# Six one-bank PSUM tiles for the block products of the last pair, and another order of VectorE's work there

## The chip, the cores and the metric

The kernel runs on one core of a Trainium2 chip. The metric is the device time of one execution in microseconds (us). Its engines are named as in the profile: PE (TensorE, matmuls; PEld is its weight load), DVE (VectorE), ACT (ScalarE), POOL (GpSimd) and SP (SyncE, which here only issues DMAs). PSUM, where PE leaves its results, has eight banks; one bank holds 512 fp32 numbers in each of the 128 partitions.

## The reference

For each of 8 batches and 12 heads an attention without softmax is computed, its heads are laid side by side to rows of 768, and a layer norm with a two-layer network and a residual follows:

```python
scores = scale * np.matmul(q, k.transpose(0, 1, 3, 2))     # q, k, v: (8, 12, 448, 64)
attn = np.maximum(scores, 0.0) ** 2 / S
x = np.matmul(attn, v)                                     # laid out as (8, 448, 768)
xn = (x - mu) / np.sqrt(var + 1e-06) * g_ln
ch = np.maximum(xn @ w_ch1, 0.0) @ w_ch2                   # 768 -> 3072 -> 768
out = x + ch
```

Inputs and output are fp32.

## The kernel before

The batches are worked on in four pairs; a pair has 896 tokens, seven tiles of 128. For each pair there is the attention (`scores`, `values`), the first layer (`ffn1`, 24 blocks of 128 hidden units, into `hT`) and the second layer (`ffn2`). The order of instructions is written out by hand: each engine works through its list in the order of the program text, and waits on semaphores for data and for buffers. For the pairs before the last, the second layer of one pair is interleaved with the attention of the next. PE is kept fed in this way almost without a gap.

The last pair has no attention to go with. There the second layer of six of its seven token tiles is computed by Strassen's scheme: `ffn2_pair` takes token tiles t and t + 4 as two block rows, the two halves of the 768 output columns as two block columns, and the two halves of the 3072 hidden units as the inner blocks. Seven block products of 12 matmuls (128x128 by 128x384) stand for eight. It is called for t = 0, 1 and 2, which are called rows here; `ffn2_last` does the token tile that is left, with 72 matmuls in three groups of 24. The sums of weight blocks (`w2_sum`) are made once; the sums of blocks of `hT` (`h_sum`, names s1, s2, s5, s6, s7) are made by DVE for one row ahead: `following("s1")` and its like issue, in the middle of one row, the sum that the next row needs, into the same tile.

The order of products in a row is 3, 2, 5, 4, 1, 6, 7. They go through PSUM as follows, with a and b for PSUM tiles:

- product 3 into a, which ACT copies to `d` (L733); product 2 into b, which DVE subtracts from `d` (L735);
- product 5 is added to what is in a, and ACT copies it to `c12` (L738); product 4 is added to b, and ACT copies it to `c21` (L742);
- product 1 into a new a; DVE makes `q_` = a + d (L745); POOL makes `d` - `c12` + `c21` (L746, L747);
- product 6 into a new b; DVE adds it to `q_` (L752); product 7 is added to a; DVE adds it to `d` (L757).

The four results of a row go through `result`: DVE scales and adds the residual in one instruction (L724), or, for `q_`, ACT scales (L727) and POOL adds (L728); `store` then issues two DMAs from SP's queue (L645) for each. The five fp32 tiles `z_sb` hold `d`, `c12`, `c21`, `q_` and the next row's `d`.

PSUM before is split for the whole kernel into two pools. `ps_sc` has three tiles of two banks (six banks) for the attention's scores and values; `ps_mm` has two tiles of one bank, for `ffn1`, `ffn2`, the seven products (m_ps) and `ffn2_last` (o_ps). In the last pair `ps_sc` is used last by `centre`, ahead of the fifth block of `ffn1`.

Of the kernel before, what the change touches and what calls it, by code (L numbers as in the profile page):

```python
# [28 lines left out]
def kernel(  # L29
# [22 lines left out]
    nc = tc.nc  # L52
    P = 128
    HP = 64
    bf16 = mybir.dt.bfloat16
    fp32 = mybir.dt.float32
# [13 lines left out]
    DH = d_model // 2  # L70
# [15 lines left out]
    hpool = ctx.enter_context(tc.tile_pool(name="h", bufs=1))  # L86
    opool = ctx.enter_context(tc.tile_pool(name="o", bufs=3))
    spool = ctx.enter_context(tc.tile_pool(name="stat", bufs=2))
    ps_sc = ctx.enter_context(tc.tile_pool(name="ps_sc", bufs=3, space=bass.MemoryType.PSUM))
    ps_mm = ctx.enter_context(tc.tile_pool(name="ps_mm", bufs=2, space=bass.MemoryType.PSUM))  # L90

    eps_sb = const.tile([P, 1], fp32)
# [215 lines left out]
    def of(blk, b=0):  # L308
        o = b % 2 * S
        return slice(o + blk[0] * HP, o + sum(blk) * HP)  # L310
# [93 lines left out]
    def centre(b, blk):  # L404
        w = blk[1] * HP
        if (b, blk) == FIRST:
            ps = ps_mm.tile([P, 512], fp32, tag="mm", name="sum_ps")[:, :w]
        else:
            ps = ps_sc.tile([P, 2, 512], fp32, tag="sc", name="sum_ps")[:, 0, :w]
        rows = [xT[b // 2][:, c, of(blk, b)] for c in range(K1)]  # L410
        if blk == FULL:
            rows = [part[b][:, i] for i in range(2)]
        for i, r in enumerate(rows):
            nc.tensor.matmul(ps, ones, r, start=(i == 0), stop=(i == len(rows) - 1))  # L414
        total = ps
        if (b, blk) != FIRST:
            total = spool.tile([P, S], fp32, tag="total", name="total_sb", bufs=1)[:, :w]
            nc.scalar.copy(total, ps)  # L418
        for c in range(K1):
            nc.vector.scalar_tensor_tensor(  # L420
                xc[b][:, c, of(blk)], total, g_mean[:, c:c + 1], xc[b][:, c, of(blk)],
                op0=ALU.mult, op1=ALU.add)
# [15 lines left out]
    def attention_block(b, blk):  # L438


        lo, hi, first = b * G, b * G + G, blk[0] == 0
        units = [lambda: transposed(lo)] if first else []

        def unit(n, part):
            squares_now()
            for i in range(4 * part, min(4 * part + 4, J), 2):
                scores(n, tuple(range(i, min(i + 2, J))), blk)
            if b == 1 and not first and part and n == hi - 1:
                transposed(hi)
            if part and n > lo:  # L450
                values(n - 1, blk)
                if not first:
                    load(n + 3, "v")
        for n in range(lo, hi):
            units.append(lambda n=n: unit(n, 0))
            if first and n + 1 < hi:
                units.append(lambda n=n: transposed(n + 1))
            units.append(lambda n=n: unit(n, 1))

        def last():  # L460
            values(hi - 1, blk)
            if b == 1 and not first:
                load(hi + 3, "v")
        units.append(last)
        units.append(lambda: centre(b, blk))
        return units
# [174 lines left out]
    def store(pair, t, cols, o, queues):  # L641
        for u, queue in enumerate(queues):
            b, j = divmod(2 * t + u, J)
            rows = out[2 * pair + b].rearrange("(p j) d -> j p d", j=J)[j]
            queue.dma_start(rows[:, cols], o[u * HP:(u + 1) * HP])  # L645
# [17 lines left out]
    def w2_sum_units():  # L663

        b = {(i, j): w2_part(i, j) for i in range(2) for j in range(2)}
        pairs = (
            ("t3", (0, 1), (1, 1), nc.vector.tensor_sub), ("t4", (1, 0), (0, 0), nc.vector.tensor_sub),
            ("t1", (0, 0), (1, 1), nc.vector.tensor_add), ("t6", (0, 0), (0, 1), nc.vector.tensor_add),
            ("t7", (1, 0), (1, 1), nc.vector.tensor_add))

        def unit(name, x, y, op, s):
            op(w2_sum[name][:, s], b[x][:, s], b[y][:, s])
        n = KH // 4
        return [lambda name=name, x=x, y=y, op=op, i=i: unit(name, x, y, op, slice(i * n, i * n + n))
                for name, x, y, op in pairs for i in range(4)]
# [23 lines left out]
    def ffn2_pair(pair, t, late, following):  # L699


        h = hT[pair].rearrange("p (kh k) (u s) -> p kh k u s", kh=2, s=P)
        left = dict(h_sum, s3=h[:, 0, :, t], s4=h[:, 1, :, t + 4])
        left["s2"], left["s5"] = h_sum["s2"], h_sum["s5"]

        def product(n, ps=None):
            first = ps is None
            if first:
                ps = ps_mm.tile([P, 512], fp32, tag="mm", name="m_ps")
            x, y = left[f"s{n}"], w2_sum[f"t{n}"]  # L710
            for ki in range(KH):
                nc.tensor.matmul(ps[:, :DH], x[:, ki], y[:, ki],  # L712
                                 start=(first and ki == 0), stop=(ki == KH - 1),
                                 skip_group_check=not first)
            return ps

        def fp():
            return late.tile([P, DH], fp32, tag="z", name="z_sb", bufs=5)

        def result(eng, z, row, half):  # L720
            u = t + 4 * row
            z3, x = z.rearrange("p (c d) -> p c d", d=D), xtok[pair][:, :, u, half * HP:(half + 1) * HP]
            if eng is nc.vector:
                eng.scalar_tensor_tensor(  # L724
                    z3, z3, rstd[pair][:, u:u + 1], x, op0=ALU.mult, op1=ALU.add)
            else:
                nc.scalar.mul(z, z, rstd[pair][:, u:u + 1])  # L727
                eng.tensor_add(z3, z3, x)  # L728
            store(pair, u, slice(half * DH, (half + 1) * DH), z, (nc.sync, nc.sync))

        a = product(3)
        d = fp()
        nc.scalar.copy(d, a[:, :DH])  # L733
        b = product(2)
        nc.vector.tensor_sub(d, d, b[:, :DH])  # L735
        product(5, a)
        c12 = fp()
        nc.scalar.copy(c12, a[:, :DH])  # L738
        product(4, b)
        following("s2")  # L740
        c21 = fp()
        nc.scalar.copy(c21, b[:, :DH])  # L742
        a = product(1)
        q_ = fp()
        nc.vector.tensor_add(q_, a[:, :DH], d)  # L745
        nc.gpsimd.tensor_sub(d, d, c12)  # L746
        nc.gpsimd.tensor_add(d, d, c21)  # L747
        result(nc.vector, c12, 0, 1)
        result(nc.vector, c21, 1, 0)
        b = product(6)  # L750
        following("s1")
        nc.vector.tensor_add(q_, q_, b[:, :DH])  # L752
        result(nc.gpsimd, q_, 1, 1)
        product(7, a)
        following("s6")
        following("s7")
        nc.vector.tensor_add(d, d, a[:, :DH])  # L757
        result(nc.vector, d, 0, 0)

    def ffn2_last(pair, t):  # L760
# [10 lines left out]
    def ffn1_units(b, blk=FULL):  # L771
        if blk == FULL:
            return [lambda ni=ni: ffn1(b, ni, blk) for ni in range(K2)]
        return [lambda: ffn1_head(b, blk)] + [lambda ni=ni: ffn1(b, ni, blk) for ni in range(3, K2)]
# [11 lines left out]
    def token_units(pair):  # L786
        return ([lambda: tokens(pair)] + [lambda t=t: statistics(pair, t) for t in range(NT)]
                + [lambda: roots(pair, 0, NT)])
# [6 lines left out]
    units, side = ffn1_units(0, BLK[0][0]), attention_block(0, BLK[0][1])  # L795
# [37 lines left out]
    units, side = ffn1_units(2 * pair), w2_sum_units()  # L833
    for i, unit in enumerate(units):
        if i == 4:
            centre(2 * pair + 1, FULL)
        unit()
        if i > 6:
            for _ in range(2):
                if side:  # L840
                    side.pop(0)()
    side = token_units(pair)
# [11 lines left out]
    for t in range(3):  # L854
        def following(name, t=t):
            if t < 2:
                h_sums_of(pair, t + 1, (name,), 0, KH)
        ffn2_pair(pair, t, late, following)
# [31 lines left out]
```

## Time and profile before

| | |
|---|---|
| median of 3 runs | 546.78 us (546.72, 546.78, 549.94) |
| profiled execution | 546.87 us |
| its span, first to last instruction | 545.0 us |
| granted TensorE clock, mean | 0.999 |
| PE busy | 533.3 us, 98% of the span |
| DVE busy | 300.2 us, 55% |
| ACT busy | 267.9 us, 49% |
| POOL busy | 119.6 us, 22% |
| products of the last pair, first matmul to first of o_ps | 487.69 to 533.29 us |

Busy time says how much of the span an engine had an instruction at work. Matmuls are pipelined: the length of one counts from its start to the end of its last result, so that two which follow each other overlap, and the pace is read from the starts. A row of the timeline gives the start, the length and the engine of a run of equal instructions, and in brackets how long the engine had been idle before, with what released it. The chain that ended last is a list of start, length, engine and line, followed back from the end of the kernel.

### The profile page before, as it was taken

The numbers are of one execution on the slowest core, as the hardware profiler recorded it, in microseconds if no ns is written. First come the engines' busy times: TensorE is split into PE (matmuls) and PEld (weight loads), VectorE is DVE, ScalarE is ACT, GpSimd is POOL, SyncE is SP. The second block draws the span as 40 slices with busy tenths as digits, with TensorE's granted clock in tenths as the row PEclk, the third lists the DMA queues.
The fourth block names the chain that finished last, engine by engine and source line by source line (L and its number), as shares of the span: only waits on it lengthen the run. The fifth ranks groups of instructions, "written<-read, shape, count | busy, mean of one in ns | idle before, by whom it ended". The sixth has DMA issues, their size and how long they took to land.

```text
span 545.0 us, 11195 instructions
## 1 busy us (share of the span) xinstructions
PE 533.3 (98%) x4720; PEld 315.5 (58%) x4720; DVE 300.2 (55%) x559; ACT 267.9 (49%) x440; POOL 119.6 (22%) x144
## 2 busy tenths in 40 slices
PE   8999999999999999999999999999999999999996
PEld 6677779655555555555555555555555555555555
DVE  5765752378886250057787432026687689035543
ACT  6967685555553444455545344445545244441110
POOL 7344111123526100003634400001230400001121
PEclk9999999999999999999999999999999999999999
DMA  9999999979999930029989980004831140001123
GB/s 197 206 205 208 211 171 185 168 126 160 164 152 146 167 42 1 0 55 147 163 149 134 176 109 1 1 14 88 151 75 31 44 102 1 1 0 26 34 58 88
DMA packets 111300, 56.64 MB, mean 104 GB/s; under 512 B 77330, under 2 KB 111250, under 8 KB 111250
## 3 DMA queue, kind: packets, MB, share of 16 engines
q0 software_dynamic: 26976, 25.50, 32.4%
q1 hardware_dynamic: 83490, 29.77, 31.8%
q8 instruction: 37, 0.61, 0.5%
q10 hardware_dynamic: 784, 0.66, 0.4%
q14 instruction: 13, 0.11, 0.1%
HBM read 51.91 MB, written 11.01 MB: 115 GB/s over the span
## 4 chain that ended last, share of the span: by engine, by line
PE 91%; DVE 2%; DMA 2%; POOL 2%; issue 1%; ACT 1%; POOLq 0%; DVEq 0%
PE h_ps L586 39%; PE o_ps L623 31%; PE sc_ps L331 7%; PE av_ps L361 6%; PE m_ps L712 5%; DMA w<-in_moe_w_ch_dram 2%; PE o_ps L766 1%; PE h_ps L608 1%; PE sum_ps L414 1%; DVE z_sb L724 1%; POOL z_sb L746 1%; ACT early L342 1%; PE tr_ps L216 0%; DVE h_sum L697 0%; POOL v_sb L126 0%
## 5 line engine op out<-in xcount | busy, mean ns | idle before, releaser
L586 PE MATMUL h_ps<-xc_sb,w 128*128 128x448 bf16 (+2 forms) x1368 | 218.9, 318 | 0.6 <-ACT early L342 0.3
L586 PEld LDWEIGHTS <-w 128*128 128x128 bf16 x1368 | 128.6, 98 | 86.6 <-issue 3.0
L623 PE MATMUL o_ps<-w,hT_sb 128*128 128x384 bf16 x1008 | 172.6, 326 | 0.0
L342 ACT ACTIVATE attn_sb<-sc_ps 128x896 bf16<-128x896 f32 (+4 forms) x150 | 126.4, 902 | 87.9 <-PE sc_ps L331 71.4
L594 ACT ACTIVATE hT_sb<-h_ps 128x448 bf16<-128x448 f32 (+2 forms) x213 | 103.0, 484 | 122.2 <-PE h_ps L586 121.7
L623 PEld LDWEIGHTS <-hT_sb 128*128 128x128 bf16 x1008 | 94.9, 98 | 74.7 <-issue 15.2
L344 DVE TENSOR_TENSOR attn_sb<-attn_sb 128x896 bf16<-128x896 bf16 x126 | 81.7, 654 | 40.2 <-ACT attn_sb L342 38.9
L565 DVE BATCH_NORM_STATS2 stats<-xtok_sb 128x6 f32<-128x384 bf16 x56 | 27.5, 533 | 34.3 <-DMA xtok_sb<-xT_sb 34.3
L397 POOL TENSOR_TENSOR part_sb<-part_sb,xT_sb 128x448 f32<-128x448 f32 x24 | 29.5, 1229 | 69.9 <-DVE xT_sb L368 62.3
L394 POOL TENSOR_TENSOR part_sb<-xT_sb 128x448 f32<-128x448 bf16 x6 | 6.6, 1105 | 172.9 <-DVE xT_sb L368 142.5
L571 DVE RECIPROCAL rstd_sb<-rstd_sb 128x1 f32<-128x1 f32 (+1 forms) x10 | 1.7, 168 | 72.4 <-ACT rstd_sb L570 72.4
L420 DVE SCALAR_TENSOR_TENSOR xc_sb<-total_sb,g_mean,xc_sb 128x448 bf16<-128x448 f32 (+2 forms) x54 | 29.0, 604 | 21.5 <-ACT total_sb L418 21.5
L634 DVE SCALAR_TENSOR_TENSOR o_sb<-o_ps,rstd_sb,xtok_sb 128x384 f32<-128x384 f32 (+1 forms) x45 | 27.0, 601 | 17.2 <-PE o_ps L623 11.0
L331 PE MATMUL sc_ps<-qT_sb,kT_sb 64*64 64x448 bf16 x504 | 35.0, 358 | 0.0
L368 DVE TENSOR_SCALAR xT_sb<-av_ps 128x896 bf16<-128x896 f32 (+2 forms) x30 | 27.0, 900 | 10.0 <-PE av_ps L361 9.8
L361 PE MATMUL av_ps<-attn_sb,v_sb 64*64 64x448 bf16 (+2 forms) x672 | 32.3, 327 | 0.0
L361 PEld LDWEIGHTS <-v_sb 64*64 64x64 bf16 x840 | 22.7, 107 | 11.9 <-issue 1.6
L384 DVE TENSOR_SCALAR xc_sb<-xT_sb,g_sb 128x448 bf16<-128x448 bf16 (+2 forms) x54 | 27.9, 567 | 1.0
L712 PEld LDWEIGHTS <-h_sum 128*128 128x128 bf16 x180 | 17.6, 98 | 12.9 <-issue 1.4
L331 PEld LDWEIGHTS <-kT_sb 64*64 64x64 bf16 x504 | 12.1, 105 | 17.6 <-issue 13.3
L126 POOL DMA_DIRECT2D v_sb<-in_v_dram x24 | 17.5, 730 | 20.2 <-PE av_ps L361 16.7
L746 POOL TENSOR_TENSOR z_sb<-z_sb 128x384 f32<-128x384 f32 x3 | 3.0, 998 | 81.7 <-DVE z_sb L745 81.7
(88 smaller groups left out, 335.8 us busy)
## 6 DMA issues: line engine op xcount, KB each, us to landing
out_dram<-o_sb SPq DMA_DIRECT2D x85, 96.0 KB, 3.0
v_sb<-in_v_dram POOLq DMA_DIRECT2D x24, 224.0 KB, 4.9
w<-in_moe_w_ch_dram POOLq DMA_DIRECT2D x12, 384.0 KB, 13.9
w<-in_moe_w_ch_dram POOLq DMA_DIRECT2D x4, 1152.0 KB, 20.0
q_sb<-in_q_dram POOLq DMA_DIRECT2D x20, 224.0 KB, 7.0
k_sb<-in_k_dram POOLq DMA_DIRECT2D x20, 224.0 KB, 5.7
out_dram<-z_sb SPq DMA_DIRECT2D x24, 96.0 KB, 2.2
hold_sb<-in_q_dram POOLq DMA_DIRECT2D x3, 224.0 KB, 11.9
```

The source lines that it names most:

```text
L331: nc.tensor.matmul(ps[cols, r, o * w:(o + 1) * w], g["k"](i)[rows, cols], g["q"](i, r)[rows, blk[0]:sum(blk), cols], start=True, stop=True)
L342: nc.scalar.activation(a, ps[:, :, :len(slots) * w], ACTF.Relu)
L344: nc.vector.tensor_mul(a, a, a)
L361: nc.tensor.matmul(ps[cols, hh, :w], v_sb[rows, pr, j * D:(j + 1) * D], g["attn"][i][rows, r, :], start=(j == 0), stop=(j == J - 1))
L384: nc.vector.tensor_scalar_mul(y, x, g_sb[:, c:c + 1])
L397: nc.gpsimd.tensor_add(part[b], part[b], x[:, c])
L420: nc.vector.scalar_tensor_tensor(xc[b][:, c, of(blk)], total, g_mean[:, c:c + 1], xc[b][:, c, of(blk)], op0=ALU.mult, op1=ALU.add)
L565: nc.vector.bn_stats(stats[:, n], xtok[pair][:, n * G:(n + 1) * G, t, :])
L586: nc.tensor.matmul(ps[:, :w], w1[:, c, ni * P:(ni + 1) * P], xc[b][:, c, of(blk)], start=(c == 0), stop=(c == K1 - 1))
L594: nc.scalar.activation(hT[pair][:, ni, o:o + w], ps[:, :w], ACTF.Relu)
L623: nc.tensor.matmul(ps[:, :DH], hT[pair][:, ki, t * P:(t + 1) * P], w2[:, ki, cols], start=(ki == 0), stop=(ki == K2 - 1))
L712: nc.tensor.matmul(ps[:, :DH], x[:, ki], y[:, ki], start=(first and ki == 0), stop=(ki == KH - 1), skip_group_check=not first)
```

## The change

- The pool `ps_sc` moves to the other end of PSUM and into an exit stack of its own, which is closed in the last pair right after `centre`. Its six banks become a pool `ps_m` with six tiles of one bank.
- Each row of `ffn2_pair` takes two tiles of `ps_m` for products 3, 2, 5 and 4, and two others for 1, 6 and 7, so that a row takes four, and the next row starts on the other two. `ffn2_last` keeps `ps_mm`.
- DVE's order within a row changes. Before: L745, `c12` (L724), `c21` (L724), s1, L752, s6, s7, L757, `d` (L724). After: L745, s1, L752, s6, `c12`, `c21`, L757, s7, `d`.
- The result `q_` (ACT L727, POOL L728, and its two stores on SP's queue) now stands ahead of the results `c12` and `c21` and their stores.

Line numbers are those of the kernel before.

```diff
-    ps_sc = ctx.enter_context(tc.tile_pool(name="ps_sc", bufs=3, space=bass.MemoryType.PSUM))
+    wide = ctx.enter_context(ExitStack())
+    ps_sc = wide.enter_context(
+        tc.tile_pool(name="ps_sc", bufs=3, space=bass.MemoryType.PSUM, side="right"))
...
-        def product(n, ps=None):
-            first = ps is None
-            if first:
-                ps = ps_mm.tile([P, 512], fp32, tag="mm", name="m_ps")
+        def banks():
+            return (ps_m.tile([P, 512], fp32, tag="m", name="m_ps")[:, :DH] for _ in range(2))
+
+        def product(n, ps, first=True):
...
-        a = product(3)
+        a, b = banks()
+        product(3, a)
         d = fp()
-        nc.scalar.copy(d, a[:, :DH])
-        b = product(2)
-        nc.vector.tensor_sub(d, d, b[:, :DH])
-        product(5, a)
+        nc.scalar.copy(d, a)
+        product(2, b)
+        nc.vector.tensor_sub(d, d, b)
+        product(5, a, False)
         c12 = fp()
-        nc.scalar.copy(c12, a[:, :DH])
-        product(4, b)
+        nc.scalar.copy(c12, a)
+        product(4, b, False)
         following("s2")
         c21 = fp()
-        nc.scalar.copy(c21, b[:, :DH])
-        a = product(1)
+        nc.scalar.copy(c21, b)
+        a, b = banks()
+        product(1, a)
         q_ = fp()
-        nc.vector.tensor_add(q_, a[:, :DH], d)
+        nc.vector.tensor_add(q_, a, d)
         nc.gpsimd.tensor_sub(d, d, c12)
         nc.gpsimd.tensor_add(d, d, c21)
+        following("s1")
+        product(6, b)
+        nc.vector.tensor_add(q_, q_, b)
+        result(nc.gpsimd, q_, 1, 1)
+        following("s6")
         result(nc.vector, c12, 0, 1)
         result(nc.vector, c21, 1, 0)
-        b = product(6)
-        following("s1")
-        nc.vector.tensor_add(q_, q_, b[:, :DH])
-        result(nc.gpsimd, q_, 1, 1)
-        product(7, a)
-        following("s6")
+        product(7, a, False)
+        nc.vector.tensor_add(d, d, a)
         following("s7")
-        nc.vector.tensor_add(d, d, a[:, :DH])
         result(nc.vector, d, 0, 0)
...
         if i == 4:
             centre(2 * pair + 1, FULL)
+            wide.close()
+            ps_m = ctx.enter_context(
+                tc.tile_pool(name="ps_m", bufs=6, space=bass.MemoryType.PSUM, side="right"))
         unit()
```

More of the change, by code (lines that the diff above doesn't have):

```diff
@@ L704, in ffn2_pair @@
         left["s2"], left["s5"] = h_sum["s2"], h_sum["s5"]
-        def product(n, ps=None):
-            first = ps is None
-            if first:
-                ps = ps_mm.tile([P, 512], fp32, tag="mm", name="m_ps")
+        def banks():
+            return (ps_m.tile([P, 512], fp32, tag="m", name="m_ps")[:, :DH] for _ in range(2))
+        def product(n, ps, first=True):
             x, y = left[f"s{n}"], w2_sum[f"t{n}"]
             for ki in range(KH):
-                nc.tensor.matmul(ps[:, :DH], x[:, ki], y[:, ki],
+                nc.tensor.matmul(ps, x[:, ki], y[:, ki],
                                  start=(first and ki == 0), stop=(ki == KH - 1),
                                  skip_group_check=not first)
-            return ps
         def fp():
```

## The prediction

> **What bounds the kernel now.** I read the page first, then the chain that ended last for the stage that the diff touches, then the timeline of PE and of DVE in that stage. The page:
>
> ```profile
> span 545.0 us, 11195 instructions
> PE 533.3 (98%) x4720; PEld 315.5 (58%) x4720; DVE 300.2 (55%) x559; ACT 267.9 (49%) x440; POOL 119.6 (22%) x144
> ```
>
> PE is busy for 98% of the span, so only time in which PE waits can be won, and the whole kernel has under 12 us of it. The question is how much lies in the three rows of products. The chain that ended last (start, length, engine, tile, line), from the first row into the second:
>
> ```profile
> 487.86 9.76 PE m_ps L712 x60
> 497.64 0.57 DVE z_sb L745
> 498.34 1.00 POOL z_sb L746
> 499.37 1.11 DVE z_sb L724
> 500.75 0.60 DVE z_sb L724
> 501.35 0.87 DVE h_sum L693
> 502.68 0.87 DVE h_sum L695
> 503.55 1.59 DVE h_sum L697
> 505.14 0.47 DVE z_sb L757
> 505.66 7.97 PE m_ps L712 x48
> ```
>
> The chain leaves PE at 497.64, runs through POOL and six DVE instructions, and comes back to PE at 505.66. It leaves by the read of product 1 (L745) and comes back by L757, the read of product 7, after which the bank of product 7 is free for product 2 of the next row. The timeline of PE shows what that costs (start, length of the run, count, and in brackets the idle time and its releaser):
>
> ```profile
> 487.69 2.11 PE L712 MATMUL m_ps<-w_sum,hT_sb 128*128 128x384 bf16 x12
> 489.64 4.06 PE L712 MATMUL m_ps<-w,h_sum 128*128 128x384 bf16 x24
> ...
> 495.49 6.01 PE L712 MATMUL m_ps<-w_sum,h_sum 128*128 128x384 bf16 x36
> 502.74 2.11 PE L712 MATMUL m_ps<-w_sum,hT_sb 128*128 128x384 bf16 x12 [1.23 <-DVE z_sb L752]
> 505.66 4.06 PE L712 MATMUL m_ps<-w,h_sum 128*128 128x384 bf16 x24 [0.81 <-DVE z_sb L757]
> ...
> 511.50 6.01 PE L712 MATMUL m_ps<-w_sum,h_sum 128*128 128x384 bf16 x36
> 518.81 2.11 PE L712 MATMUL m_ps<-w_sum,hT_sb 128*128 128x384 bf16 x12 [1.29 <-DVE z_sb L752]
> 521.01 4.06 PE L712 MATMUL m_ps<-w,h_sum 128*128 128x384 bf16 x24
> ...
> 526.86 6.01 PE L712 MATMUL m_ps<-w_sum,h_sum 128*128 128x384 bf16 x36
> 533.29 8.02 PE L766 MATMUL o_ps<-w,hT_sb 128*128 128x384 bf16 x72 [0.42 <-DVE z_sb L752]
> ```
>
> All waits of PE are at the start of a row, on the two reads L752 and L757 that free the two banks. Inside a row PE has none, though products 5, 4 and 7 wait there for a read of the bank that they add to.
>
> **The pace without a wait.** From 487.69 to 489.64 twelve matmuls start with no wait, 1.95 us for a product, 0.1625 us each. A row of seven products is then 7 x 1.95 = 13.65 us. What each start is late by is the start less the start of the run before and its count times 0.1625:
>
> - Row 2, product 3: 495.49 + 36 x 0.1625 = 501.34; it starts at 502.74, 1.40 late. Product 2: 502.74 + 1.95 = 504.69; it starts at 505.66, 0.97 late.
> - Row 3, product 3: 511.50 + 5.85 = 517.35; 518.81, 1.46 late. Product 2: 518.81 + 1.95 = 520.76; 521.01, 0.25 late.
> - `ffn2_last`: 526.86 + 5.85 = 532.71; 533.29, 0.58 late.
>
> The sum is 4.66 us. As a cross-check, the stage from 487.69 to 533.29 is 45.60 us, less three rows of 13.65 (40.95) leaves 4.65. This is more than the idle time in brackets (3.75), because a pipelined matmul still counts as busy for some 0.16 us after the next one could have started.
>
> **The change part by part.**
>
> *Six banks.* A row takes four banks and the next row starts on two that it did not touch, so products 3 and 2 of rows 2 and 3 no longer wait for L752 and L757. The same holds for `ffn2_last`: it stays on `ps_mm`, which is last read by the evictions of `ffn1` before row 1. In the changed program's instruction order these matmuls carry no wait on DVE or ACT at all; the first product of row 1 waits only for `centre`'s matmuls, which stand ahead of all but four blocks of `ffn1`. The gain is the whole 4.66 us, provided that no other wait stands behind the removed ones.
>
> *What else PE waits for.* Product 5 waits for ACT's read of product 3, product 4 for DVE's read of product 2 (L735), product 7 for L745; each has the product in between, 1.95 us, as cover, against a read of 0.48 (ACT, the row below) or 0.56 us (DVE). The first two sums of a row (s2, s5) are made a row ahead. The sums s1, s6 and s7 that move on DVE are needed by products 1, 6 and 7 of the next row, 13.65 us after the products whose end they wait for. In product 1's case that leaves some 11 us; if this cover were gone PE would wait for the 0.94 us that one sum takes.
>
> ```profile
> L733 ACT COPY z_sb<-m_ps x3: 479/479/480, 489.9 to 521.0; 128x384 f32<-128x384 f32 x3
> ```
>
> *DVE's order.* No DVE instruction is added or removed. What is queued now behind L757 is s7 and the result `d`, and behind these L735 of the next row, for which product 4 waits. So the one place where DVE could still be late is L735. The rows of DVE and then of POOL, first row into second:
>
> ```profile
> 497.64 0.56 DVE L745 TENSOR_TENSOR z_sb<-m_ps,z_sb 128x384 f32<-128x384 f32 x1 [2.14 <-PE m_ps L712]
> 499.37 1.98 DVE L724 SCALAR_TENSOR_TENSOR z_sb<-z_sb,rstd_sb,xtok_sb 128x384 f32<-128x384 f32 x2 [1.17 <-POOL z_sb L746]
> 501.27 0.94 DVE L693 TENSOR_TENSOR h_sum<-hT_sb 128x1536 bf16<-128x1536 bf16 x1
> 502.14 0.54 DVE L752 TENSOR_TENSOR z_sb<-z_sb,m_ps 128x384 f32<-128x384 f32 x1
> ...
> 503.48 1.66 DVE L697 TENSOR_TENSOR h_sum<-hT_sb 128x1536 bf16<-128x1536 bf16 x1
> ...
> 505.64 0.62 DVE L724 SCALAR_TENSOR_TENSOR z_sb<-z_sb,rstd_sb,xtok_sb 128x384 f32<-128x384 f32 x1
> 507.87 0.56 DVE L735 TENSOR_TENSOR z_sb<-z_sb,m_ps 128x384 f32<-128x384 f32 x1 [1.61 <-PE m_ps L712]
> ```
>
> ```profile
> 498.33 1.00 POOL L746 TENSOR_TENSOR z_sb<-z_sb 128x384 f32<-128x384 f32 x1 [63.12 <-DVE z_sb L745]
> 499.41 1.00 POOL L747 TENSOR_TENSOR z_sb<-z_sb 128x384 f32<-128x384 f32 x1
> 503.41 0.91 POOL L728 TENSOR_TENSOR z_sb<-z_sb,xtok_sb 128x384 f32<-128x384 f32 x1 [3.01 <-ACT z_sb L727]
> ```
>
> The moved sum s1 now fills the 1.17 us in which DVE waited for POOL. Today the same nine instructions run from 497.64 to 505.64 + 0.62 = 506.26. In the changed kernel product 2 of row 2 ends at about 501.34 + 2 x 1.95 = 505.24, and product 4 may start at 507.19. Even if DVE were as late as today, L735 would end at 506.26 + 0.56 = 506.82, and 0.37 us are left. That is the value I take: cost 0. The bound from the other side: DVE and POOL slow each other when they overlap, as L697 with 1.66 us beside POOL's L728 against 0.94 for the like sum L693. If they never overlapped from 498.20 on, there would be POOL's 1.00 + 1.00 + 0.91 and DVE's 3 x 0.94 + 3 x 0.62 + 2 x 0.54 = 5.76, in sum 8.67, to 506.87, and L735 to 507.43. With 0.1 us of gap for each of eleven instructions (POOL's L747 starts 0.08 after the end of L746) it is 508.5, so product 4 would be up to 1.3 us late in each of rows 2 and 3: a cost of 0 to 2.6 us. I take the end 0, since the observed chain has the same work in it and is the nearer row.
>
> *The results' order on SP's queue.* Nothing is added: eight DMAs a row. The stores of `c12` and `c21` now stand behind `q_`'s, which wait for POOL's L728, some 1 to 2 us later than today. Who waits for a landed store is the next row's `z_sb` tiles:
>
> ```profile
> out_dram<-z_sb SPq DMA_DIRECT2D x24, 96.0 KB, 2.2
> ```
>
> `q_` is made about 0.2 us after the end of product 6, scaled, added by POOL and stored by about 3 + 2.2 us after it; its tile is wanted by `c12` of the next row, four products (7.8 us) after it. Hidden, with some 2.5 us to spare; were it not, ACT's copy would be late first, and product 7 only behind it. After the last row these stores precede `ffn2_last`'s own in SP's queue. The end of the timeline:
>
> ```profile
> 537.39 0.62 DVE L634 SCALAR_TENSOR_TENSOR o_sb<-o_ps,rstd_sb,xtok_sb 128x384 f32<-128x384 f32 x1 [3.03 <-PE o_ps L766]
> ...
> 538.91 3.34 SPq L645 DMA_DIRECT2D out_dram<-o_sb  x3
> ...
> 541.35 0.42 DVE L634 SCALAR_TENSOR_TENSOR o_sb<-o_ps,rstd_sb,xtok_sb 128x192 f32<-128x192 f32 x1 [1.56 <-PE o_ps L766]
> ```
>
> The last stores are issued after 541.77, when the queue has long caught up. The 3.2 us from there to the end of the span stay as they are: at most 0.9 us could be won, because SP's first o_sb store goes out 0.90 after DVE's end for it (537.39 + 0.62, 538.91), and I take 0.
>
> *The pools' places.* Attention and `ffn1` get other banks for the first 487 us; nothing in their order changes. Cost 0, with a bound that no row gives apart from the matmul pace, which is equal in both banks of `ps_mm` (products 3 and 2 above both at 1.95).
>
> **The sum.** 546.87 (profiled execution, 1.87 around its span of 545.0) − 4.66 = 542.2 us. The median of the runs, 546.78, is 0.09 below that execution, so it moves to 542.1; I give 542.2. That is 0.85% less. 1% is about what a measurement of this kernel can tell from no change, and 1% would be 5.47 us, so my forecast lies within it, just.
>
> **The rivals.**
>
> *DVE becomes the bound* (0.10). Product 4 waits for L735 in rows 2 and 3, by the 1.3 us above at the worst: 542.2 + 0.5 to 2.6, 542.7 to 544.8. For it: DVE and POOL hold each other up (1.66 against 0.94), and s1 now runs right beside L746. Against it: today's chain, with POOL's waits in it, would be in time.
>
> *More than the waits is won* (0.14). The last stores gain the 0.9 us above as well, because row 3's stores are out sooner: 541.3 or less. For it: SP's first o_sb store is late today. Against: the last one is not.
>
> *The change does not do what it says* (0.03). The wait on L752 hides another, such as the sum or a store, that ends at the same time: 546.8. Against it: product 3 of row 2 reads `hT_sb`, which `ffn1` finished before row 1, and a weight sum made before that.
>
> *Slower: the granted clock falls in the products* (0.04). PE then works through 57 us with no gap, from six banks in turn. Three stretches, with the clock as the third number from the right:
>
> ```profile
> 446.00:487.00 41.00, 41.00 (x219) 21.20 (x217) 20.48 (x46) 19.91 (x38) 0.00 (x0) 1.00 0.00 1
> 501.00:503.00 2.00, 0.77 (x6) 0.39 (x4) 2.00 (x4) 0.28 (x1) 0.00 (x0) 1.00 0.40 86
> 543.00:545.00 2.00, 0.00 (x0) 0.00 (x0) 0.00 (x0) 0.00 (x0) 0.00 (x0) 0.71 0.17 44
> ```
>
> PE worked 41 us without a gap at a clock of 1.00; the clock falls only where PE has stopped, to a mean of 0.71. At 0.71 the 40.95 us of products would take 57.7, 16.7 more: 558.9 us. The gain is eaten up at a clock of 0.90 (40.95 / 0.90 = 45.5), and the kernel is 1% slower below 0.80. Against it: the clock stays at 1.00 at the start of row 2 (501 to 503), where PE idles longest.
>
> The Trainium skill, "TensorE: Matmul & The Clock Gate", section "A second HAM failure mode: psum-queue depth-cycling", speaks against this change: a kernel that cycled through PSUM banks idled so often between groups of matmuls that the clock swung between 4/8 and full. By that rule, at half clock throughout, the products would take 40.95 us more. The trace of before does not show it with two banks in turn, and no run before shows six.
>
> The remaining 0.69 is the forecast.
>
> **How the numbers follow.** Faster by over 1% is the second rival, 0.14, and 0.02 of the forecast's own scatter: 0.16. Slower by over 1% is the fourth, 0.04. Within 1% is the rest, 0.80. The range: downwards the 0.9 us of the stores and the 0.09 of the median, 541.2; upwards the DVE rival to most of its length, 544.5. It leaves out the third and the fourth rival and about half of the second, some 0.15.
>
> **What would show it.** Right: no idle time ahead of PE's runs of L712 after 488, a row of 13.65 us from product 3 to product 3, the first o_ps matmul at 487.69 + 40.95 = 528.64, and a span near 540.3. The chain that ended last should then stay on PE through the products. DVE late: idle time ahead of runs of 12 at product 4, released by L735. Clock: a granted clock under 1.00 in the stretch 488 to 528. The forecast is wrong if the first product starts elsewhere than 487.7, as then the pools' new places cost something, or if PE waits for `h_sum` or ACT's copies.

## The result and the profile after

The median of the changed kernel is 542.09 us over 8 runs, against 546.83 for the kernel before over 8 runs: a ratio of 0.9914, with a 95% interval of 0.9891 to 0.9936. That is 4.74 us, where 4.66 was forecast. The interval leaves no doubt about the sign; the size, 0.86%, is under the 1% that the prediction set as its bound, though the interval reaches 1.1%.

The profiled execution of the changed kernel took 545.38 us (span 543.5) and lost some 3 us in its first 17 us, long ahead of the products (the last section returns to it); the other seven spans are 540.1 to 540.4 us. So its times after the start are read as differences.

In the changed kernel's lines, L714 is the product (L712 before), L769 the matmul of `ffn2_last` (L766), L748 the read of product 1 (L745), L753 and L759 the reads that free a row's banks (L752, L757), L737 the read of product 2 (L735), L695, L697 and L699 the sums s1, s6 and s7, L725 the scaled result, L749, L750 and L729 POOL's instructions. The timeline of PE after, the same stretch as before (start, length, count):

```profile
490.86 2.11 PE L714 MATMUL m_ps<-w_sum,hT_sb 128*128 128x384 bf16 x12
492.81 4.06 PE L714 MATMUL m_ps<-w,h_sum 128*128 128x384 bf16 x24
496.71 2.11 PE L714 MATMUL m_ps<-w_sum,hT_sb 128*128 128x384 bf16 x12
498.66 6.01 PE L714 MATMUL m_ps<-w_sum,h_sum 128*128 128x384 bf16 x36
504.51 2.11 PE L714 MATMUL m_ps<-w_sum,hT_sb 128*128 128x384 bf16 x12
...
518.16 2.11 PE L714 MATMUL m_ps<-w_sum,hT_sb 128*128 128x384 bf16 x12
...
531.81 8.02 PE L769 MATMUL o_ps<-w,hT_sb 128*128 128x384 bf16 x72
```

No row has a bracket: PE does not idle. A row takes 504.51 − 490.86 = 13.65 us, the next 518.16 − 504.51 = 13.65, the third 13.65. From the first product to the first matmul of `ffn2_last` it is 40.95 us, 4.65 less than the 45.60 of before. The chain that ended last, which before left PE for DVE and POOL around every row start, now stays on it to the end:

```profile
491.03 40.95 PE m_ps L714 x252
531.98 7.87 PE o_ps L769 x72
```

The stretch of the products: busy time by engine (PE, PEld, DVE, ACT, POOL), then the granted clock, the DMA share and GB/s:

```profile
490.90:531.80 40.90, 40.90 (x253) 24.62 (x252) 23.88 (x31) 6.71 (x13) 10.78 (x9) 1.00 0.18 39
```

PE is busy for all of it, at a clock of 1.00. Seven products in 13.65 us are 1.95 us each, the pace of before without its waits.

### The profile page after: what moved, and what is told of

It is laid out like the page before. It is cut to its first block, busy times and chain, and to the rows that moved or that the text cites. A ratio compares the mean times of both kernels' runs of the same rounds, so it can differ in the third digit from the quotient of the medians.

```text
span 543.5 us, 11194 instructions
## 1 busy us (share of the span) xinstructions
PE 537.1 (99%) x4720; PEld 318.8 (59%) x4720; DVE 300.3 (55%) x559; ACT 268.0 (49%) x440; POOL 121.1 (22%) x144
## 4 chain that ended last, share of the span: by engine, by line
PE 97%; ACT 1%; DVE 0%; issue 0%
PE h_ps L588 39%; PE o_ps L625 31%; PE m_ps L714 8%; PE sc_ps L333 7%; PE av_ps L363 6%; PE h_ps L610 1%; PE o_ps L769 1%; PE tr_ps L218 1%; ACT early L344 1%; PE sum_ps L416 1%; PE idle_ps L204 1%; PE busy_ps L308 0%; DVE xT_sb L370 0%; ACT early L221 0%; DVE o_sb L636 0%
## 5 line engine op out<-in xcount | busy, mean ns | idle before, releaser
L714 PEld LDWEIGHTS <-h_sum 128*128 128x128 bf16 x180 | 17.6, 98 | 11.6
L749 POOL TENSOR_TENSOR z_sb<-z_sb 128x384 f32<-128x384 f32 x3 | 4.2, 1387 | 81.9 <-DVE z_sb L748 72.5
## 6 DMA issues: line engine op xcount, KB each, us to landing
hold_sb<-in_q_dram POOLq DMA_DIRECT2D x3, 224.0 KB, 11.7
```

The lines of the kernel that those rows point to most:

```text
L714: nc.tensor.matmul(ps, x[:, ki], y[:, ki], start=(first and ki == 0), stop=(ki == KH - 1), skip_group_check=not first)
```

## The experiments

Theory A is the one of the prediction: PE waited only because a bank was read late. Theory B says that the new order of DVE brings the gain (and that the old order would only move the wait); theory B' that only the number of banks does. `banks_alone`, `order_alone`, `order_late` and `side_only` ran beside the same 15 runs of the kernel before (546.74 us), the other four beside 13 (546.66).

### Banks alone

```diff
-        following("s1")
-        product(6, b)
-        nc.vector.tensor_add(q_, q_, b)
-        result(nc.gpsimd, q_, 1, 1)
-        following("s6")
         result(nc.vector, c12, 0, 1)
         result(nc.vector, c21, 1, 0)
+        product(6, b)
+        following("s1")
+        nc.vector.tensor_add(q_, q_, b)
+        result(nc.gpsimd, q_, 1, 1)
         product(7, a, False)
-        nc.vector.tensor_add(d, d, a)
+        following("s6")
         following("s7")
+        nc.vector.tensor_add(d, d, a)
         result(nc.vector, d, 0, 0)
```

> The changed kernel with the old order of DVE and of the results: six one-bank tiles, but c12 and c21 (L724) ahead of s1, L752, s6, s7, L757. Theory A (a bank that is read late is all that PE waited for): no product waits for L752 or L757, and L735 of the next row, with today's chain of 8.6 us from L745, ends about 19.1 us after the row's start against product 4 at 19.5; so a row takes 13.65 us and the time is 542.1 us. Theory B (the order of DVE's work brings the gain, and the old order would only move the wait): idle time ahead of product 4, released by L735, by up to some 1 us in rows 2 and 3, 543 to 545 us.

Measured: 542.0 us, ratio 0.9912 [0.9899, 0.9926]: the whole gain. Its timeline of PE, the starts of row 1, row 2 and `ffn2_last`:

```profile
487.50 2.11 PE L714 MATMUL m_ps<-w_sum,hT_sb 128*128 128x384 bf16 x12
...
501.15 2.11 PE L714 MATMUL m_ps<-w_sum,hT_sb 128*128 128x384 bf16 x12
503.10 4.06 PE L714 MATMUL m_ps<-w,h_sum 128*128 128x384 bf16 x24
507.00 2.11 PE L714 MATMUL m_ps<-w_sum,hT_sb 128*128 128x384 bf16 x12
...
528.45 7.78 PE L769 MATMUL o_ps<-w,hT_sb 128*128 128x384 bf16 x69
```

and of DVE, whose order is that of before:

```profile
497.45 0.56 DVE L748 TENSOR_TENSOR z_sb<-m_ps,z_sb 128x384 f32<-128x384 f32 x1 [2.14 <-PE m_ps L714]
499.17 1.98 DVE L725 SCALAR_TENSOR_TENSOR z_sb<-z_sb,rstd_sb,xtok_sb 128x384 f32<-128x384 f32 x2 [1.16 <-POOL z_sb L749]
...
505.44 0.62 DVE L725 SCALAR_TENSOR_TENSOR z_sb<-z_sb,rstd_sb,xtok_sb 128x384 f32<-128x384 f32 x1
505.98 0.55 DVE L737 TENSOR_TENSOR z_sb<-z_sb,m_ps 128x384 f32<-128x384 f32 x1
```

Rows of 13.65 us again. DVE works late here: L737 has no idle time ahead of it, starts behind `d`'s result at 505.98 and ends at 506.53, 0.47 us before product 4 starts at 507.00. This is the case that the prediction worked out for DVE (as late as today, 0.37 us to spare), and it holds; in row 3 the margin is 1.06 us (L737 ends at 519.59, product 4 starts at 520.65). Theory B falls. `banks_alone` has the old order of the results and their stores too, so with the banks that order is worth nothing either.

### The order alone

In the kernel before: `c12` and `c21` go behind s6, s1 ahead of product 6, and the read of product 7 ahead of s7, as in the changed kernel; the products keep the two tiles of `ps_mm`.

> The kernel before with the new order of DVE and of the results, but the two tiles of ps_mm for the products. Theory A, from the changed kernel's trace: L752 ends 12.45 us after the start of its row, ahead of the next row's product 3 at 13.65, so that wait is gone; L757 ends at 16.30, against product 2 at 15.60, so product 2 of rows 2 and 3 starts 0.75 late each. 542.1 + 1.5 = 543.6 us. Theory B' (only more banks remove the waits, whatever the order): as before, 546.8 us.

Measured: 543.61 us, ratio 0.9943 [0.993, 0.9955]. Its timeline of PE (here the line of the read of product 7 is L756):

```profile
495.38 6.01 PE L712 MATMUL m_ps<-w_sum,h_sum 128*128 128x384 bf16 x36
501.24 2.11 PE L712 MATMUL m_ps<-w_sum,hT_sb 128*128 128x384 bf16 x12
503.94 4.06 PE L712 MATMUL m_ps<-w,h_sum 128*128 128x384 bf16 x24 [0.59 <-DVE z_sb L756]
...
518.34 4.06 PE L712 MATMUL m_ps<-w,h_sum 128*128 128x384 bf16 x24 [0.59 <-DVE z_sb L756]
```

Product 3 of row 2 starts at 501.24, with no wait. Product 2 starts at 503.94 instead of 503.19, 0.75 late as expected, because L756 stands behind `c12` and `c21` (the two L724) in DVE's order and is over only at 503.88:

```profile
501.63 1.79 DVE L724 SCALAR_TENSOR_TENSOR z_sb<-z_sb,rstd_sb,xtok_sb 128x384 f32<-128x384 f32 x2
503.34 0.54 DVE L756 TENSOR_TENSOR z_sb<-z_sb,m_ps 128x384 f32<-128x384 f32 x1
```

The order alone brings 3.1 of the 4.7 us.

### Another order, with two banks

```diff
+        product(7, a)
         following("s6")
+        nc.vector.tensor_add(d, d, a[:, :DH])
         result(nc.vector, c12, 0, 1)
         result(nc.vector, c21, 1, 0)
-        product(7, a)
-        nc.vector.tensor_add(d, d, a[:, :DH])
         following("s7")
```

This is against the order alone.

> Two tiles of ps_mm as before and another order of DVE: L745, s1, L752, s6, L757, then c12, c21, s7, d. Theory A: L757 is over about 14.8 us after the start of the row, ahead of product 2 at 15.60, and L752 at 12.5 ahead of product 3 at 13.65, so two banks are enough and nothing waits: 542.1 us, as with six banks. Theory B' (only more banks remove the waits): 546.8 us, or at best what the new order alone gives, 543.6.

Measured: 542.0 us, ratio 0.9913 [0.9899, 0.9926], the same as with six banks. The timeline of DVE, and below it that of PE:

```profile
499.40 0.56 DVE L750 TENSOR_TENSOR z_sb<-z_sb,m_ps 128x384 f32<-128x384 f32 x1 [0.53 <-PE m_ps L712]
499.87 1.75 DVE L695 TENSOR_TENSOR h_sum<-hT_sb 128x1536 bf16<-128x1536 bf16 x1
501.54 0.54 DVE L754 TENSOR_TENSOR z_sb<-z_sb,m_ps 128x384 f32<-128x384 f32 x1
```

```profile
501.15 2.11 PE L712 MATMUL m_ps<-w_sum,hT_sb 128*128 128x384 bf16 x12
503.10 4.06 PE L712 MATMUL m_ps<-w,h_sum 128*128 128x384 bf16 x24
```

The bank of product 6 is read (L750) by 499.96, ahead of 501.15; that of product 7 (L754) by 502.08, ahead of 503.10. Theory B' falls: two banks are enough if they are read in time.

### The pool's place alone

`ps_sc` is given `side="right"` in the kernel before, and nothing else is changed.

> The kernel before, with the pool ps_sc at the other end of PSUM and nothing else, so that every matmul ahead of the last pair writes to the banks that it has in the changed kernel. Theory A: no change, 546.8 us, with the waits of before at the row starts (a row of about 15 to 16 us). Rival (the places of the banks bring part of the gain): less than 546 us, and the first product earlier than 487.7 us after the start.

Measured: 546.63 us over 10 runs, ratio 0.9997 [0.9988, 1.0006]: nothing. The first product starts at 487.62, and the waits of before are there with the same 1.23 and 0.81 us:

```profile
487.62 2.11 PE L713 MATMUL m_ps<-w_sum,hT_sb 128*128 128x384 bf16 x12
...
502.65 2.11 PE L713 MATMUL m_ps<-w_sum,hT_sb 128*128 128x384 bf16 x12 [1.23 <-DVE z_sb L753]
505.57 4.06 PE L713 MATMUL m_ps<-w,h_sum 128*128 128x384 bf16 x24 [0.81 <-DVE z_sb L758]
```

### Four banks

`bufs=6` becomes `bufs=4` in the pool `ps_m`.

> The changed kernel with four tiles in the pool ps_m instead of six. The next row starts on the two tiles of its own row's products 3, 2, 5 and 4 one row before, which ACT has read 7.8 us earlier (L742 stands behind product 4, three products ahead of the next row's start). Theory A: 542.1 us, no wait. Rival (the distance of six banks matters, PE waits for a bank that is read one row earlier): more than 543 us.

Measured: 541.97 us, ratio 0.9914 [0.9899, 0.9928]. Six banks bring nothing over four.

### How much cover DVE has left

In the changed kernel, s7 is made n more times in rows 1 and 2 (n = 1, 2, 3):

```diff
         following("s7")
+        for _ in range(n):
+            following("s7")
         result(nc.vector, d, 0, 0)
```

> The changed kernel with the sum s7 made twice by DVE in rows 1 and 2 (one more instruction of 0.94 us each, ahead of the result d; the same numbers are written). It measures the cover of L735. From the changed kernel's trace d ends at 508.56, the end of product 2 lets L735 start at 508.68, L735 ends at 509.24 and product 4 starts at 510.36. With some 0.87 us more L735 ends at about 510.0: product 4 is not late, 542.1 us. Rival (the cover is already used up, DVE paces the rows): each added 0.9 us shows twice, 543.8 us.

> The changed kernel with two more sums s7 in rows 1 and 2. L735 ends about 0.5 us after product 4 could start, in rows 2 and 3: 542.1 + 1.1 = 543.2 us, with idle time ahead of product 4 released by L735. Rival (DVE already paces the rows): 545.6 us; rival (more cover than worked out): 542.1 us.

> The changed kernel with three more sums s7 in rows 1 and 2. Product 4 is about 1.4 us late in rows 2 and 3: 542.1 + 2.8 = 544.9 us. Rival (DVE already paces the rows): 547.3 us.

Measured: 542.5 us (542.19 to 543.13), 543.4 and 545.44; ratios 0.9925 [0.991, 0.994], 0.994 [0.9923, 0.9956] and 0.9979 [0.9969, 0.9988]. With one more sum the timeline of PE has no idle time ahead of any product, and rows of 13.65 us:

```profile
488.71 2.11 PE L714 MATMUL m_ps<-w_sum,hT_sb 128*128 128x384 bf16 x12
...
502.36 2.11 PE L714 MATMUL m_ps<-w_sum,hT_sb 128*128 128x384 bf16 x12
```

That execution took 543.13 us because its first product starts 1.2 us later than the 487.4 to 487.6 of the other experiments. It lost this time long before the products, where PE waited for a transfer of weights (`four_banks` has the same matmuls at 34.27, with no wait):

```profile
35.54 1.16 PE L588 MATMUL h_ps<-xc_sb,w 128*128 128x192 bf16 x12 [0.79 <-DMA w<-in_moe_w_ch_dram]
```

Two of the other three executions, 542.19 and 542.24 us, are within 0.15 us of the changed kernel's median; what made the last one 542.77 is not known. With two and with three more the wait is where it was expected, at product 4, in rows 2 and 3. The timeline of PE with two, with three, and that of DVE with three:

```profile
503.17 4.06 PE L714 MATMUL m_ps<-w,h_sum 128*128 128x384 bf16 x24
507.77 2.11 PE L714 MATMUL m_ps<-w_sum,hT_sb 128*128 128x384 bf16 x12 [0.54 <-DVE z_sb L737]
```

```profile
503.09 4.06 PE L714 MATMUL m_ps<-w,h_sum 128*128 128x384 bf16 x24
508.68 2.11 PE L714 MATMUL m_ps<-w_sum,hT_sb 128*128 128x384 bf16 x12 [1.53 <-DVE z_sb L737]
```

```profile
503.71 3.92 DVE L699 TENSOR_TENSOR h_sum<-hT_sb 128x1536 bf16<-128x1536 bf16 x4
...
508.08 0.55 DVE L737 TENSOR_TENSOR z_sb<-z_sb,m_ps 128x384 f32<-128x384 f32 x1
```

With two, product 4 starts at 507.77 instead of 503.17 + 3.90 = 507.07, 0.70 late; with three it was 1.69 late (508.68 against 506.99). Both are more than expected (some 0.5 and 1.4), because s7 made several times over, into one and the same tile, takes DVE 0.98 us a time (3.92 for four), not the 0.87 that I had put in. The 0.87 is the distance of two sums into different tiles: s6 and s7 start at 502.61 and 503.48 in the kernel before. Two sums, 1.96 us, made it 0.70 late, and three, 2.94 us, 1.69 late, so the cover of L737 in the changed kernel is about 1.25 us. Within it, more work on DVE costs nothing; beyond it, it costs its full length in each row.

## Why the prediction was right

*The sum.* The working by starts (4.66 us) was met to 0.1 us; the sum of the idle times in brackets (3.75) would have been 1 us too small. Each term is gone, with no wait in its place.

*The six banks.* Right that they remove the whole wait, and alone (542.0 us). What the prediction did not see is that they are not needed for it: with two banks, a read of product 7 ahead of the two results removes it too. The part on the order weighed only whether it costs anything. In truth the order of the change alone buys 3.1 us of the same gain, and that of `order_late` all of it; with the banks, neither the old order nor the new one changes the time.

*DVE.* Cost 0 was right, but its working undervalued the new order. It put `d`'s end as late as before, 8.62 us after L745 started, with 0.37 us of cover. That is what the banks alone give (0.47), not the order that was forecast. In the changed kernel:

```profile
500.81 0.56 DVE L748 TENSOR_TENSOR z_sb<-m_ps,z_sb 128x384 f32<-128x384 f32 x1 [2.14 <-PE m_ps L714]
501.29 0.95 DVE L695 TENSOR_TENSOR h_sum<-hT_sb 128x1536 bf16<-128x1536 bf16 x1
502.76 0.55 DVE L753 TENSOR_TENSOR z_sb<-z_sb,m_ps 128x384 f32<-128x384 f32 x1 [0.53 <-PE m_ps L714]
503.24 1.75 DVE L697 TENSOR_TENSOR h_sum<-hT_sb 128x1536 bf16<-128x1536 bf16 x1
...
507.95 0.61 DVE L725 SCALAR_TENSOR_TENSOR z_sb<-z_sb,rstd_sb,xtok_sb 128x384 f32<-128x384 f32 x1
508.68 0.56 DVE L737 TENSOR_TENSOR z_sb<-z_sb,m_ps 128x384 f32<-128x384 f32 x1
```

The work ends at 508.56, 7.75 us after L748, since s1 fills DVE's wait for POOL. L737 then starts 0.12 us later, when product 2 is done as well, and ends at 509.24, 1.12 us ahead of product 4 (510.36): more than twice the margin of the banks alone. The upper bound of 2.6 us, with DVE and POOL never at once, was far from what happened.

*The stores and the tail.* Cost 0 and no gain, as taken: spans of 540.1 to 540.4 us are the 540.3 that was named, so the rival in which the last stores win 0.9 us did not come. From the first matmul of `ffn2_last` to the end of the span it is 11.7 us, as before. The rival's premise, that row 3's stores are out sooner, did not hold either:

```profile
535.91 0.62 DVE L636 SCALAR_TENSOR_TENSOR o_sb<-o_ps,rstd_sb,xtok_sb 128x384 f32<-128x384 f32 x1 [2.69 <-PE o_ps L769]
```

```profile
538.92 1.87 SPq L647 DMA_DIRECT2D out_dram<-o_sb  x3
```

SP's first store of `o_sb` now goes out 2.39 us after DVE's end for it, against 0.90 before; by the last store the queue has caught up.

*The places of the banks.* 0, by `side_only`. The first product of the profiled execution starts at 490.86 and not at 487.7, which the prediction had named as a sign that the places cost something. They do not: with the same places, `banks_alone` starts at 487.50. The sign was badly chosen, as it is also moved by the start of the kernel.

*The granted clock.* It stayed at 1.00 through 40.9 us without a gap, and the pace of 1.95 us a product shows the same. The 57 us without a gap that the prediction names are too few: PE is busy for 98.3 of the 98.5 us from 441.5 to 540.0. The Trainium skill's rule in "TensorE: Matmul & The Clock Gate", section "A second HAM failure mode: psum-queue depth-cycling", does not bear here: PE has no idle time between the groups, with two (`order_late`), four or six banks. In the kernel before it has some at the row starts, up to 1.29 us, and there too the clock is 1.00, and the two products behind one such wait run from 505.66 to 509.55, 1.95 us each.

## What to carry to other kernels

A pipelined engine's lateness is read from the starts of its runs against its own pace (4.66 us here), not from the idle time that the trace gives in brackets (3.75). Where PE waits for a bank, look first at which read frees it and what that reader does ahead of it: moving the read forward in its engine's order can be worth as much as more banks. Once the wait is gone, find the next instruction that the reader would make late and measure its cover by adding work to it.

## What was not expected of the hardware

DVE and POOL held each other up in the new order too. In the changed kernel POOL's L749 runs beside s1 in row 1 and beside no sum in row 3:

```profile
501.50 1.59 POOL L749 TENSOR_TENSOR z_sb<-z_sb 128x384 f32<-128x384 f32 x1 [63.12 <-DVE z_sb L748]
...
528.80 1.00 POOL L749 TENSOR_TENSOR z_sb<-z_sb 128x384 f32<-128x384 f32 x1 [9.41 <-issue]
```

It takes 1.59 us in the first and 1.00 in the second. In row 1 it ends at 503.09, about one length of 1.00 after the end of s1 (502.24), so it seems to have waited rather than run slowly. The Trainium skill, "SBUF — State Buffer", section "SBUF: two separate sides", says so: of a DVE instruction with two inputs in SBUF and a POOL instruction that reads SBUF, the one that starts first holds the shared ports for its whole length. The trace agrees, within 0.15 us. So does L753, one of whose inputs is in PSUM: it starts beside L749 at 502.76 and takes 0.55 us, as L752 did alone (0.54). The other way round, L697 starts at 503.24 beside POOL's L750 (503.17 to 504.17), takes 1.75 us instead of 0.95, and ends 0.82 us after L750 does.

The 3 us at the start of the profiled execution are a slower pace of PE that the granted clock does not show. Three equal small matmuls and the stretch from 8 to 17 us (PE, PEld, DVE, ACT, POOL, then the granted clock, the DMA share and GB/s), first in the profile of before and then in that of after:

```profile
6.37 0.34 PE L306 MATMUL busy_ps<-ones 128*128 128x128 bf16 x3
```

```profile
7.06 0.50 PE L308 MATMUL busy_ps<-ones 128*128 128x128 bf16 x3
```

```profile
8.00:17.00 9.00, 7.31 (x214) 5.66 (x214) 7.48 (x17) 7.89 (x14) 5.45 (x9) 1.00 1.26 205
```

```profile
8.00:17.00 9.00, 8.54 (x148) 6.45 (x144) 4.91 (x12) 5.40 (x9) 5.19 (x9) 1.00 1.25 204
```

The clock reads 1.00 in both, but the same matmuls take half as long again after, and PE gets through 148 matmuls in this stretch where it did 214 before, while being busier. The slow pace ends by 17.75 us, where the same three take 0.34 us again:

```profile
17.75 0.34 PE L308 MATMUL busy_ps<-ones 128*128 128x128 bf16 x3
```

So early a stretch is touched by the change only through the place of `ps_sc`, and the profiles of the experiments with the same place (`side_only`, `banks_alone`, `four_banks` and the three with more sums) have 0.34 us for these matmuls by 7 us. Why the slow pace lasted so long in this one execution was not tried.
